# Attention backward on one core: giving nine of the dk stores another distribution over the DMA engines

## The chip, the core and the metric

The kernel runs on one core of one Trainium2 chip. The metric is the device time of one execution in microseconds (us). The core has 16 DMA engines, which all its loads and stores share. A DMA issued by GpSimd (POOL in the profile) goes through the "software" queue q0, one issued by SyncE (SP) through the "hardware" queue q1.

## The reference

Attention with one query per head, and its gradients, in bf16: 2 x 32 = 64 heads, 8192 keys, D = 128.

```python
def _fwd_reference(q, k, v):                 # q: 2,32,1,128   k, v: 2,32,8192,128
    scale = q.shape[-1] ** -0.5
    scores = jnp.einsum("bhqd,bhkd->bhqk", q, k) * scale
    p = _softmax(scores, axis=-1)
    return jnp.einsum("bhqk,bhkd->bhqd", p, v)

def reference(q, k, v, grad_out):            # returns out, dq, dk, dv
    out, vjp = jax.vjp(_fwd_reference, q, k, v)
    return (out, *vjp(grad_out))
```

Per head, k and v are read and dk and dv written, 2 MB each: 537 MB in all. With 128 partitions, one partition's share of a head (a "row") is 64 keys x 128 x 2 bytes = 16 KB, contiguous in memory.

## The kernel before

PE transposes and multiplies the k and v tiles of one head while the next heads are loaded. DVE overwrites a tile with its gradient, and the tile is then stored from where it lies. Loads are issued by SyncE, stores by GpSimd (in the last head in small pieces by SyncE). Twelve tiles are in use in turn, so a load waits for the store that empties its tile.

```python
FIRST = 6
SPREAD = range(4, 60, 7)
...
load_eng = nc.sync
store_eng = nc.gpsimd
...
    def by_rows(eng, dst, src, rows):
        p = 0
        for m in rows:
            pin(eng.dma_start(out=dst[p : p + m], in_=src[p : p + m], max_dma_last_dim=NT * D))
            p += m
...
        if r0:                         # r0 = FIRST for q
            pin(store_eng.inc_swdge_sem([], [], mode="reset_dge_cursor"))
            pin(store_eng.dma_start(out=qd_nat[:r0, w, :], in_=rows[:r0], max_dma_last_dim=D))
        pin(load_eng.dma_start(out=qd_nat[r0:BH, w, :], in_=rows[r0:BH]))
...
            if w == 0 and i in SPREAD:                       # dk of heads 4, 11, ... 53
                by_rows(store_eng, dst, h.tile[w], (P - 2, 2))
            else:
                eng = load_eng if len(ends) > 1 else store_eng
                pin(eng.dma_start(out=dst[:, b0:b1, :], in_=h.tile[w][:, b0:b1, :]))
```

In the packet records a plain store of 128 rows gives each engine 8 rows, and the eight spread stores divide 126 rows by 14 engines, so that two engines get next to nothing. Where a copy over fewer than 16 engines begins is kept by a cursor of the software queue (the prediction quotes the rule). The program resets it at the start and moves it to 6 by a load of six rows.

## Time and profile before

| | before |
|---|---|
| time, median of 4 runs | 1280.99 us (1280.43 to 1281.8) |
| span of the profiled run | 1280.2 us |
| PE busy | 1190.2 us, 93% |
| last two stores issued (compute over) | 1270.29 us |
| DMA, mean over the span | 421 GB/s |

The page gives busy time per engine. In rows of digits each digit is a fortieth of the span, in tenths busy. A window line gives a stretch, its length, the busy time of PE, PEld (weight loads), DVE, ACT and POOL with instruction counts, the PE clock, the DMA share (1.00 is all 16 engines) and GB/s. A DMA share of 0.06 is one engine.

### The profile page before, as it was taken

The page shows a single profiled execution, that of the slowest core. Times are in us where ns is not written, and L with a number is a line of the kernel's source. Part 1 is how long each engine was busy: PE and PEld are TensorE (multiplying, and loading weights), DVE is VectorE, ACT ScalarE, POOL GpSimd, SP SyncE. Part 2 cuts the span into 40 slices and gives each one's busy share as a digit, 9 for nine tenths or more (in the row PEclk, how much of TensorE's full clock was granted, in tenths as well). Part 3 has the DMA queues.
Part 4 walks back from the last instruction along what each step waited for, and adds up shares of the span by engine and source line. Part 5 has one row for each costly group of instructions (what it writes and reads, how often), then busy time and mean ns, then how long its engine had stood idle before and what let it go on. Part 6 is the DMA issues. An engine that isn't in the chain of part 4 may idle for free.

```text
span 1280.2 us, 32473 instructions
## 1 busy us (share of the span) xinstructions
PE 1190.2 (93%) x14148; PEld 810.6 (63%) x14148; DVE 1025.8 (80%) x2256; ACT 975.3 (76%) x641; POOL 76.0 (6%) x143
## 2 busy tenths in 40 slices
PE   6999999999999999999999999999999999999994
PEld 5666666666666666666666666666666666666662
DVE  2888887888877888888888878788778888888885
ACT  6777777778777777777777777787777777777771
POOL 0000000000000000000000000000000000000000
PEclk9999999999999999999999999999999999999996
DMA  9999999999999999999999999999999999999996
GB/s 392 423 428 428 428 427 429 430 426 429 427 430 425 414 427 429 428 423 428 428 429 419 425 428 426 427 421 427 427 423 421 427 429 428 420 425 428 428 411 273
DMA packets 40155, 539.03 MB, mean 421 GB/s; under 512 B 5196, under 2 KB 5196, under 8 KB 6476
## 3 DMA queue, kind: packets, MB, share of 16 engines
q1 hardware_dynamic: 20172, 272.70, 50.1%
q0 software_dynamic: 19840, 264.25, 49.0%
q8 instruction: 110, 1.80, 0.5%
q14 instruction: 33, 0.27, 0.1%
HBM read 268.47 MB, written 268.47 MB: 419 GB/s over the span
## 4 chain that ended last, share of the span: by engine, by line
PE 59%; DVE 16%; ACT 10%; issue 10%; DMA 4%; POOL 0%; SPq 0%; ACTq 0%; POOLq 0%; DVEq 0%
PE tp L194 24%; PE acc L372 15%; ACT ev L196 9%; PE raw L208 9%; DVE kvt L427 6%; PE sw L228 4%; DVE sel L395 4%; DMA out_dram<-kvt 3%; DVE rows L221 3%; PE sw L315 3%; PE sw L178 2%; PE acc L409 2%; ACT E_f L271 1%; DVE sel L389 1%; DVE E_pad L280 1%
## 5 line engine op out<-in xcount | busy, mean ns | idle before, releaser
L196 ACT COPY ev<-tp 128x2048 bf16<-128x2048 bf16 x512 | 954.5, 1865 | 275.6 <-PE tp L194 268.9
L427 DVE TENSOR_TENSOR kvt<-qb,pair 128x2048 bf16<-128x2048 bf16 x512 | 616.8, 1216 | 0.2
L194 PE MATMUL tp<-ident_bf,kvt 128*128 128x128 bf16 x8192 | 544.4, 220 | 0.0
L194 PEld LDWEIGHTS <-kvt 128*128 128x128 bf16 x8192 | 482.4, 99 | 81.6 <-issue 80.7
L208 PE MATMUL raw<-ev,qdT 128*32 128x512 bf16 x2048 | 205.2, 391 | 1.5 <-ACT ev L196 1.5
L372 PE MATMUL acc<-kvt,E_pad 128*64 128x512 bf16 x1024 | 160.2, 393 | 24.5 <-DVE E_pad L280 24.5
L372 PE MATMUL acc<-kvt,dS_pad 128*64 128x512 bf16 x1024 | 159.8, 393 | 0.1
L228 PEld LDWEIGHTS sw<-sel,rows 128*128 128x128 f32 x1024 | 124.7, 192 | 52.4 <-DVE sel L395 25.9
L395 DVE SCALAR_TENSOR_TENSOR sel<-acc,diag,sel 128x128 f32<-128x128 f32 x384 | 134.8, 351 | 13.6
L208 PEld LDWEIGHTS <-qdT 128*32 128x32 bf16 x2048 | 53.1, 93 | 136.6 <-issue 131.8
L228 PE MATMUL sw<-sel,rows 128*128 128x16 f32 x1024 | 137.1, 266 | 0.0
L445 POOL DMA_DIRECT2D out_dram<-kvt x118 | 63.3, 536 | 1094.0 <-DVE kvt L427 555.7
L221 DVE COPY rows<-raw 128x512 f32<-128x512 f32 x128 | 88.6, 692 | 22.4 <-PE raw L208 22.4
L280 DVE CAST E_pad<-E_f 128x64 bf16<-128x64 f32 x64 | 12.5, 195 | 80.3 <-ACT E_f L271 80.3
L372 PEld LDWEIGHTS <-E_pad 128*64 128x64 bf16 x1024 | 36.1, 108 | 49.9 <-DVE E_pad L280 35.7
L178 PE MATMUL sw<-ident_bf,qdT 128*128 128x128 bf16 x128 | 28.5, 223 | 38.2 <-DVE mp L240 38.2
L246 DVE TENSOR_REDUCE gm<-sw 1x1 f32<-1x128 f32 x64 | 17.9, 279 | 55.4 <-PE sw L244 55.4
L315 PEld LDWEIGHTS sw<-ld,ones 128*128 128x128 f32 x256 | 38.1, 188 | 29.7 <-issue 15.0
L372 PEld LDWEIGHTS <-dS_pad 128*64 128x64 bf16 x1024 | 36.4, 108 | 22.3 <-DVE dS_pad L358 1.0
L315 PE MATMUL sw<-ld,ones 128*128 128x1 f32 x256 | 49.1, 261 | 0.0
L409 PE MATMUL acc<-ones,sel 128*128 128x1 f32 x256 | 43.3, 239 | 5.3 <-DVE sel L395 5.3
L389 DVE TENSOR_SCALAR sel<-acc,diag 128x128 f32<-128x128 f32 x128 | 43.8, 342 | 0.0
(49 smaller groups left out, 377.1 us busy)
## 6 DMA issues: line engine op xcount, KB each, us to landing
out_dram<-kvt POOLq DMA_DIRECT2D x118, 2048.0 KB, 40.6
kvt<-in_v_dram SPq DMA_DIRECT2D x64, 2048.0 KB, 19.1
kvt<-in_k_dram SPq DMA_DIRECT2D x63, 2048.0 KB, 19.4
out_dram<-kvt POOLq DMA_DIRECT2D x8, 2016.0 KB, 44.9
out_dram<-kvt SPq DMA_DIRECT2D x8, 512.0 KB, 10.9
kvt<-in_k_dram SPq DMA_DIRECT2D x2, 512.0 KB, 4.3
kvt<-in_k_dram SPq DMA_DIRECT2D x1, 1024.0 KB, 6.9
out_dram<-kvt POOLq DMA_DIRECT2D x8, 32.0 KB, 44.3
```

The costliest lines, as they stand in the source:

```text
L194: pin(nc.tensor.transpose(tp[:, t, :], src[:, c * CH + t, :], ident_bf[:]))
L196: pin(nc.scalar.copy(out=ev[:], in_=tp[:]))
L208: nc.tensor.matmul(h.raw[g * SW : (g + 1) * SW, :], lhsT=qdT[:, w, q0 : q0 + SW], rhs=ev[:, g * QT : (g + 1) * QT, :].rearrange("p n d -> ...
L221: pin(nc.vector.tensor_copy(out=h.rows[:], in_=h.raw[:]))
L228: nc.tensor.matmul(h.score[w].rearrange("p (n t) -> p n t", t=QT)[:, :, t], lhsT=h.rows[:, t * P : (t + 1) * P], rhs=sel4[:].rearrange("p ...
L315: nc.tensor.matmul(out, lhsT=ones[:].to_broadcast([P, P]), rhs=col, start=True, stop=True)
L372: nc.tensor.matmul(h.acc[w][g : g + CW, :], lhsT=wts[:, n0 : n0 + CW], rhs=rows[:, n0 : n0 + QT, :].rearrange("p n d -> p (n d)"), start=( ...
L389: nc.vector.tensor_scalar(out=h.sel[:], in0=block, scalar1=diag[:, 0:1], scalar2=None, op0=ALU.mult)
L395: nc.vector.scalar_tensor_tensor(out=h.sel[:], in0=block, scalar=diag[:, b : b + 1], in1=h.sel[:], op0=ALU.mult, op1=ALU.add,)
L409: nc.tensor.matmul(h.acc[w][:, 0:1], lhsT=h.sel[:], rhs=ones[:], start=True, stop=True)
L427: nc.vector.tensor_tensor(out=h.tile[w][:, n0 : n0 + CH, :].rearrange("p n (e t) -> p n e t", t=2), in0=h.qb[w][:] .rearrange("p (e t) -> ...
L445: pin(eng.dma_start(out=dst[:, b0:b1, :], in_=h.tile[w][:, b0:b1, :]))
```

## The change

Its intent, as its short description says, is to take work from one engine, number 4, in seven stores (120 rows over 15 engines), and from engines 7 and 8 in two late ones (112 rows). SyncE stores the seven rows left over. The last row goes in pieces of 9 and 8 columns (3 and 2 in the last store), evidently chosen so that 15 + 9 + 8 = 32 brings the cursor back (in the last, 15 + 3 + 2 = 20 would set it to 9, from where 14 engines would leave out 7 and 8).

```diff
-FIRST = 6
-SPREAD = range(4, 60, 7)
+FIRST = 5
+ONE = {4: 9, 12: 9, 20: 9, 28: 9, 36: 9, 44: 9, 52: 3}
+TWO = (57, 61)
...
-            if w == 0 and i in SPREAD:
-                by_rows(store_eng, dst, h.tile[w], (P - 2, 2))
+            if w == 0 and i in ONE:
+                by_rows(store_eng, dst, h.tile[w], (P - 8,))
+                by_rows(load_eng, dst, h.tile[w], (7,), P - 8)
+                a = 2 * ONE[i]
+                for eng, cols in (
+                    (store_eng, slice(0, a - 1, 2)),
+                    (store_eng, slice(1, a - 2, 2)),
+                    (load_eng, slice(a - 1, NT)),
+                ):
+                    pin(eng.dma_start(out=dst[P - 1 :, cols, :], in_=h.tile[w][P - 1 :, cols, :]))
+            elif w == 0 and i in TWO:
+                by_rows(store_eng, dst, h.tile[w], (P - 16, 2))
+                by_rows(load_eng, dst, h.tile[w], (7, 7), P - 14)
```

(by_rows also gets a first row as a parameter; lines are joined here.)

More of the change, by code (lines that the diff above doesn't have):

```diff
@@ L83, in slot_of, with by_rows @@
         return n if n < NTILE else slot_of(i - NTILE // 2, 1 - w)
-    def by_rows(eng, dst, src, rows):
-        p = 0
+    def by_rows(eng, dst, src, rows, p=0):
         for m in rows:
@@ L440, in outer @@
             dst = (dv_v if w else dk_v)[i]
-            if w == 0 and i in SPREAD:
-                by_rows(store_eng, dst, h.tile[w], (P - 2, 2))
+            if w == 0 and i in ONE:
[7 more added lines that the diff above has]
+                ):
+                    pin(
+                        eng.dma_start(
+                            out=dst[P - 1 :, cols, :], in_=h.tile[w][P - 1 :, cols, :]
+                        )
+                    )
+            elif w == 0 and i in TWO:
+                by_rows(store_eng, dst, h.tile[w], (P - 16, 2))
+                by_rows(load_eng, dst, h.tile[w], (7, 7), P - 14)
             else:
```

## The prediction

> **What bounds the kernel now.** I read the page's busy shares first, then the windows of 19.4 us (one head each), then the end of the run in small windows, then the issues and SyncE's waits.
>
> ```profile
> PE 1190.2 (93%) x14148; PEld 810.6 (63%) x14148; DVE 1025.8 (80%) x2256; ACT 975.3 (76%) x641; POOL 76.0 (6%) x143
> ...
> PEclk9999999999999999999999999999999999999996
> DMA  9999999999999999999999999999999999999996
> ```
>
> PE and the DMA engines are both full until the last slice. The windows decide between them (columns: stretch, its length, busy us of PE, PEld, DVE, ACT, POOL, clock, DMA share, GB/s):
>
> ```profile
> 75.40:94.80 19.40, 18.43 (x223) 12.58 (x221) 15.94 (x36) 15.19 (x11) 1.06 (x2) 1.00 1.01 428
> ...
> 405.90:425.40 19.50, 18.54 (x225) 12.59 (x221) 16.04 (x36) 15.29 (x11) 1.13 (x2) 1.00 1.00 409
> ...
> 1203.20:1222.60 19.40, 18.44 (x225) 12.59 (x221) 15.93 (x36) 15.18 (x11) 1.06 (x2) 1.00 1.01 430
> ```
>
> PE does the same 18.4 us of work in every window, also where the DMA rate drops to 409 GB/s: PE never waits for data. The chain of waits agrees: its marker, one 1.86 us eviction per head, recurs every 19.445 us. So compute takes about 17 + 64 x 19.445 = 1261.5 us and a short tail, and no DMA change can shorten that. A head moves 8.39 MB, which at 19.445 us asks for 431 GB/s; the DMA engines give about 427. They fall behind a little all the way, and what is left of that is paid at the end:
>
> ```profile
> 1268.00:1270.00 2.00, 0.89 (x3) 0.63 (x3) 0.92 (x3) 0.00 (x0) 0.00 (x0) 0.50 0.96 389
> 1270.00:1272.00 2.00, 0.01 (x1) 0.00 (x0) 0.35 (x2) 0.00 (x0) 0.00 (x0) 0.50 0.54 217
> 1272.00:1274.00 2.00, 0.00 (x0) 0.00 (x0) 0.00 (x0) 0.00 (x0) 0.00 (x0) 0.50 0.47 182
> 1274.00:1276.00 2.00, 0.00 (x0) 0.00 (x0) 0.00 (x0) 0.00 (x0) 0.00 (x0) 0.50 0.08 30
> 1276.00:1278.00 2.00, 0.00 (x0) 0.00 (x0) 0.00 (x0) 0.00 (x0) 0.00 (x0) 0.50 0.06 25
> ...
> 1270.29 1.88 SPq L528 DMA_DIRECT2D out_dram<-nat  x2
> ```
>
> Compute is over at 1270.3, when SyncE issues the last two small stores. From 1274 to 1278 the DMA share is 0.06, which is one engine of 16 (1/16 = 0.0625). **One straggling DMA engine sets the end.** Its last packet ends at 1278.15 in the packet records, the span 2.0 us later.
>
> To know the engines I chained the packet records: they name no engine, but a 16 KB packet takes 611 ns and the next on the same engine starts 607 ns after it, so sixteen chains can be followed. This is my reconstruction (chains can swap where two coincide), but it fits every packet count. It says:
> - In each of the eight spread stores 14 chains carry 18 packets of 8 KB (nine rows) and two carry only 4-byte ones, then one row each. So these two are relieved by 7 rows, 8 times.
> - Exactly one engine is slow from the first store on: its packets take 13 to 60 ns too long, 44 us in the run. It is one of the relieved two. The other one has 27 us of long packets, but in bursts, when it has run ahead and starts a new load at once; an ordinary engine has 4 to 14.
> - The 110 fetches of PE instructions (queue q8, about 0.96 us each) go in turn to 8 engines, 14 each, 13 us. The slow engine is not among them, the other relieved one is.
> - Idle time up to the end: slow engine 12 us, the other relieved one 20, the engines without fetches 6 to 15, those with fetches mostly under 2. The straggler is a fetching engine with 13 us of long packets; its sisters end at 1273.3 to 1274.4.
>
> **What the Trainium skill says.** "DMA: Bandwidth & Descriptors", section "Why a DMA increments its semaphore by 16 and not by 1": a copy uses the largest k up to 16 that divides both sides' slowest dimension; the hardware queue uses the lowest-numbered k engines, the software queue k consecutive ones from a round-robin cursor; and some direct software copies take all 16 regardless. The trace agrees for 126 rows: 14 chains, two left out. No trace yet shows 120, 112 or a copy of nine columns. The same page, "Issuing engines are not separate DMA queues": moving a store to SyncE adds no bandwidth; here both queues fill the same 16 chains. The same page, "Latency and other measured facts", calls engines 7 and 15 the usual slow ones; here one engine is slow, and the change's own choice says that its number is 4.
>
> **The change part by part,** in rows of 16 KB against an even split, 0.611 us a row, if the cursor moves as the rule says.
> - Before: the first small load of 6 rows puts the cursor at 6; 126 rows go to 6-15 and 0-3, 2 rows to 4 and 5. Eight times: engines 4 and 5 have -56 rows, the others +8.
> - After, seven stores: cursor 5, 120 rows on 15 engines, all but 4; then 9 and 8 column pieces bring it round (15 + 9 + 8 = 32) to 5. Seven rows by SyncE go to engines 0-6, the rest of the last row (12 to 15 KB) to engine 0. Engine 4: 7 x (-8 + 1) = -49. Engines 1-3, 5, 6: +7. Engine 0: about +12. Others 0.
> - Two stores of 112 rows: the title wants 7 and 8 left out; by the rule 16 divides 112, so I count 7 rows on each engine, two rows to two engines, 14 by SyncE to 0-6: +2 for 0-6, -1 or -2 for 7-15. With 7 and 8 left out it would be -14 for these two and 4 for 0-6.
>
> Change against before: engine 4 +9 rows (5.5 us of its 12 idle). Engine 5 +65 rows, 40 us, against 20 us idle plus some 20 us of burst waits (27 less an ordinary 7): it just fits. Engines 7-15: 9 or 10 rows less, -6 us. Engines 1-3 and 6 +1 row, 0 about +6: up to 4 us, inside the idle of engines without fetches. A fetching engine at +1 row or engine 5 ends near 1274; if the straggler is among 7-15, it ends near 1272. The floor is the last small store: on engines that keep up it lands at 1273.2. So the last packet is at about 1274, the span 1276, and with the 0.5 us that timed runs are above this span, **1276.7 us**. All gain is in the 4 us of the lone engine.
>
> Costs: GpSimd issues 16 more small copies; it is 6% busy, so they are hidden. The 256-byte pieces are 17 packets a store, nothing. SyncE's rows stand in its queue between two loads, behind a wait for an earlier store:
>
> ```profile
> SPq L100 <- DMA out_dram<-kvt: 1136.8, 116, 27.5
> ...
> out_dram<-kvt POOLq DMA_DIRECT2D x118, 2048.0 KB, 40.6
> kvt<-in_v_dram SPq DMA_DIRECT2D x64, 2048.0 KB, 19.1
> ```
>
> They are issued a store's 40 us later than now and land behind the load just queued (19 us), so the next load starts about 10 us later in nine heads. The engines stay busy with the store queue, which has several stores waiting. The last load (head 63) is issued at 1211.5, lands at about 1230 and is first used at about 1241; issued at about 1222 it lands near 1233, since nothing is queued before it. No PE stall.
>
> **The rivals.** First, *the cursor does not move as planned*. A nine-column copy has a single counting dimension, and the skill's exception (all 16 engines) may apply; then the pieces leave the cursor alone, and the left-out engine walks 4, 3, 2, 1, 0, 15, 14. Engine 4 has then +1 row instead of -56: 57 rows at 0.63 us are 36 us, less 12 idle: 24 us behind 1273, a span near 1299 with one engine alone for over 20 us. For it: the old code split rows in two to get this behaviour, the new pieces don't. Against: 9 + 8 and 3 + 2 columns make sense only if the author had seen the cursor move by them. I give it 0.35 to 0.4. Second, *SyncE's queue becomes the wait*: a load late by more than its lead stalls PE, which then moves the whole end. The lead of the last load is about 10 us; I expect 0 to 4 us, 1277 to 1281. Third, *engine 5 or a sister becomes the straggler*, if the burst waits were not slack: up to 20 us, again near 1295; the trace speaks against it, as its first 397 us have only 2 us of long packets. Fourth, *all balanced but nothing gained*: some engine among 0-6 carries what the straggler carried, 1280.
>
> **Range and chances.** With 0.6 the plan works: 1275 to 1280. With 0.4 one engine is overloaded: 1290 to 1300. The middle of this mixture is 1278; eight in ten need both modes, 1274.5 to 1299.5. Two per cent faster (1255) is below the compute floor of 1275: 0.01. Slower than 1306 needs an overload and a PE stall together: 0.04.
>
> **What would show it.** Right: PE 18.4 us in every window, compute over at 1270.3, no window at a share of 0.06 after 1274, in each of the seven stores one chain with 4-byte packets only, and it is the slow one. Wrong: the share stays at 0.06 for 20 us (an engine overloaded; the chain's packets of over 611 ns tell whether it is engine 4), or PE windows under 18 us (loads late), or compute's last store after 1271.

## The result, and the profile after

| | before | after |
|---|---|---|
| time, median of 4 runs | 1280.99 us | 1304.08 us (1301.69 to 1304.16) |
| ratio | | 1.0175 (95%: 1.0158 to 1.0193) |
| span of the profiled run | 1280.2 us | 1302.4 us |

Ratios are computed from means: the mean time of one kernel's fast runs over that of the other's in the same rounds, so not quite the ratio of the medians. The changed kernel is slower by 23 us, inside two per cent and outside the predicted range.

The page of after, the lines that answer to those of before:

```profile
PE 1194.4 (92%) x14148; PEld 812.0 (62%) x14148; DVE 1025.4 (79%) x2256; ACT 975.3 (75%) x641; POOL 79.5 (6%) x151
...
PEclk9999999999999999999999999999999999999995
DMA  9999999999999999999999999999999999999965
GB/s 391 421 428 429 427 425 428 428 428 428 419 429 428 427 426 419 428 429 425 422 414 429 429 424 425 410 428 427 426 427 425 429 425 429 417 420 426 415 238 205
```

PE does the same work. The DMA rate is that of before until the last two slices. Windows of before that the prediction did not show:

```profile
1222.60:1242.10 19.50, 18.53 (x225) 12.59 (x221) 16.03 (x36) 15.28 (x11) 1.06 (x2) 1.00 0.96 406
1242.10:1261.50 19.40, 16.56 (x136) 9.62 (x132) 16.28 (x37) 7.58 (x6) 1.06 (x2) 0.82 0.83 352
1261.50:1280.90 19.40, 2.58 (x14) 1.42 (x14) 7.60 (x15) 0.00 (x0) 0.00 (x0) 0.57 0.55 224
```

The same windows of after, and its end:

```profile
1203.20:1222.60 19.40, 18.02 (x219) 12.52 (x217) 15.33 (x36) 14.77 (x11) 1.06 (x2) 1.00 1.01 429
1222.60:1242.10 19.50, 18.54 (x225) 12.59 (x221) 16.02 (x36) 15.29 (x11) 1.06 (x2) 1.00 0.86 350
1242.10:1261.50 19.40, 14.44 (x151) 9.45 (x148) 12.35 (x29) 10.65 (x6) 1.83 (x3) 0.91 0.85 327
1261.50:1280.90 19.40, 15.28 (x107) 8.29 (x106) 16.60 (x35) 4.04 (x4) 0.55 (x1) 0.77 0.59 237
...
1285.00:1290.00 5.00, 0.32 (x1) 0.13 (x1) 0.40 (x3) 0.00 (x0) 0.00 (x0) 0.50 0.30 114
1290.00:1295.00 5.00, 0.00 (x0) 0.00 (x0) 0.00 (x0) 0.00 (x0) 0.00 (x0) 0.50 0.06 27
1295.00:1300.00 5.00, 0.00 (x0) 0.00 (x0) 0.00 (x0) 0.00 (x0) 0.00 (x0) 0.50 0.06 26
```

Two things are seen. From 1290 to 1300 one engine works alone. And PE, which before had 2.58 us left to do after 1261.5, has 15.28 us left now, so it has lost time. The group of PE's transposes says to whom (page; the last column is PE's idle time just before them and its releaser), before and then after:

```profile
L194 PE MATMUL tp<-ident_bf,kvt 128*128 128x128 bf16 x8192 | 544.4, 220 | 0.0
```

```profile
L194 PE MATMUL tp<-ident_bf,kvt 128*128 128x128 bf16 x8192 | 545.4, 220 | 12.7 <-DMA kvt<-in_v_dram 11.0
```

PE waits 11.0 us for late v tiles. The last two stores are issued at 1285.70 (timeline of SyncE in after), 15.4 us later than before:

```profile
1285.70 3.07 SPq L543 DMA_DIRECT2D out_dram<-nat  x2
```

So of the 22 us between the spans some 15 are late compute. The rest is a longer tail behind it, most of it the lone engine.

**Which engine.** I chained the packet records of after into sixteen engines as for before. A left-out engine shows as a chain that carries only 4-byte packets of a 120-row store. In the seven stores it was a different chain each time. The first was the slow chain. The fifth was the one that carries SyncE's 12 KB rest of the last row, which is engine 0 if the hardware queue uses the lowest engines. The first five lie among the chains that carry the 256-byte column pieces, the last two do not. That is the walk 4, 3, 2, 1, 0, 15, 14: the cursor moves by 15 in each store and not at all by the pieces, whose data landed on the same nine and eight chains every time. The slow engine was relieved once and then carried one row above even in each of six stores. This is a reconstruction, and it ends at 1235 us. So I tested it.

### The profile page after: what moved, and what is told of

It reads as the page before. It is cut to its first block, busy times and chain, and to the rows that moved or that the text cites. A ratio compares the mean times of both kernels' runs of the same rounds, so it can differ in the third digit from the quotient of the medians.

```text
span 1302.4 us, 32523 instructions
## 1 busy us (share of the span) xinstructions
PE 1194.4 (92%) x14148; PEld 812.0 (62%) x14148; DVE 1025.4 (79%) x2256; ACT 975.3 (75%) x641; POOL 79.5 (6%) x151
## 4 chain that ended last, share of the span: by engine, by line
PE 55%; DVE 15%; DMA 10%; ACT 9%; another core or an unknown queue 6%; issue 2%; SPq 0%; ACTq 0%; DVEq 0%
PE tp L194 23%; PE acc L372 14%; DMA kvt<-in_v_dram 9%; PE raw L208 8%; ACT ev L196 8%; DVE kvt L427 6%; PE sw L228 4%; DVE sel L395 4%; DVE rows L221 3%; PE sw L315 2%; PE sw L178 2%; PE acc L409 1%; ACT E_f L271 1%; DVE sel L389 1%
## 5 line engine op out<-in xcount | busy, mean ns | idle before, releaser
L372 PEld LDWEIGHTS <-dS_pad 128*64 128x64 bf16 x1024 | 36.6, 108 | 22.3 <-issue 0.9
```

The lines of the kernel that those rows point to most:

```text
L372: nc.tensor.matmul(h.acc[w][g : g + CW, :], lhsT=wts[:, n0 : n0 + CW], rhs=rows[:, n0 : n0 + QT, :].rearrange("p n d -> p (n d)"), start=( ...
```

## Experiments

Each of the four calls ran on another chip (14, 6, 4 and 12), with runs of before on the same chip. So between calls the ratios can be compared better than the medians.

**Call 1: the cursor.** The tool is a tiny software copy from q into unused memory. It has two counting dimensions, as the first small load has, and so should take as many engines as it has rows and move the cursor:

```diff
+    moved = nc.dram_tensor("moved", (512, D), BF16, kind="Internal").ap()
+    def move_cursor(m):
+        pin(store_eng.dma_start(out=moved[put[0] : put[0] + m, : D // 2], in_=rows[:m, : D // 2], max_dma_last_dim=D // 4))
+        put[0] += m
```

e1_back: after the pieces of each 120-row store, tiny copies of 9 and 8 rows.

```diff
+                move_cursor(9); move_cursor(8)
```

> The changed kernel with two tiny software copies more after each of the seven 120-row stores, of 9 and of 8 rows of q into unused memory, each with two counting dimensions, as the first small load has them. Theory A (the column pieces do not move the software queue's cursor, so the left-out engine walks 4, 3, 2, 1, 0, 15, 14): 9 + 8 = 17 slots undo the walk by one, the same engine is left out in all seven stores, and the time falls from 1304 to 1276 - 1280 us, with compute over near 1270 and no lone engine for longer than 4 us. Rival B (SyncE's rows delay the loads, or engine 5 is the straggler, whatever the cursor does): stays at 1300 - 1306. Rival C (the pieces do move the cursor by 17): 17 more spoil a plan that worked, another walk, 1300 or more, with the left-out chain moving on by one each time.

e2_sixteen, its control:

```diff
+                move_cursor(8); move_cursor(8)
```

> As e1_back, but the two tiny copies have 8 and 8 rows: 16 slots, which bring a cursor of 16 back to where it was. It is the control for what the tiny copies do by themselves. Theory A: the walk of the changed kernel stays, 1302 - 1306 us. If the tiny copies helped by anything else than the cursor, e1_back and e2_sixteen would be equal.

e4_five:

```diff
-FIRST = 5
+FIRST = 6
+                move_cursor(9); move_cursor(8)
```

> As e1_back, but the first small load has 6 rows in place of 5, so that the one engine left out seven times is the next one, engine 5. Theory A with the slow engine being number 4: engine 4 has one row more per store than an even share (SyncE's rows begin at engine 0) and is skipped in none, against one skip in the changed kernel: 8 rows or 5 us more, 1305 - 1312 us. If any engine left out seven times would do, or if engine 5 were the straggler: 1276 - 1285.

e3_plain:

```diff
-            if w == 0 and i in ONE:
+            if False:
...
-            elif w == 0 and i in TWO:
+            elif False:
```

> All dk stores as plain 128-row copies over 16 engines, by the software queue, no rows on SyncE. Theory A: in the changed kernel the slow engine ended with about as many rows as an even split gives it, so without any relief the time is about the same, 1300 - 1306 us. Rival B (SyncE's rows in the queue of the loads cost the 20 us): without them 1280 or less.

| | median | ratio to before (95%) |
|---|---|---|
| e1_back | 1292.44 us | 1.0093 (1.0051 to 1.0134) |
| e2_sixteen | 1306.72 us | 1.0199 (1.0164 to 1.0234) |
| e4_five | 1316.9 us | 1.0278 (1.0248 to 1.0308) |
| e3_plain | 1293.86 us | 1.0103 (1.0074 to 1.0133) |

e1_back and e2_sixteen differ by one slot of the cursor per store, and by 14.3 us. In the chains of e1_back one and the same engine, the slow one, is left out in all seven stores. In e2_sixteen it is a different one from store to store, and only the first is the slow one. So **the pieces do not move the cursor, and that costs 14 us**: theory A's cause holds. e4_five is slower again: the same relief given to engine 5 does not help. The loss against e2_sixteen is 10 us, twice the 5 us that I expected from after.

A count that needs no chains agrees. The slow engine shows in 8 KB packets of 313 to 341 ns, where 309 is usual. The seven 120-row stores have 0, 10, 8, 6, 13, 10 and 12 of these in after, 0, 10, 10, 5, 14, 13 and 11 in e2_sixteen, at most 2 each in e1_back, and 5 to 15 each in e4_five.

PE's waits tell where the late compute comes from. e3_plain has no rows on SyncE and no relief; e1_back has all of SyncE's rows and the relief (pages, e3_plain first):

```profile
L194 PE MATMUL tp<-ident_bf,kvt 128*128 128x128 bf16 x8192 | 544.4, 220 | 11.5 <-DMA kvt<-in_v_dram 8.6
```

```profile
L205 PE MATMUL tp<-ident_bf,kvt 128*128 128x128 bf16 x8192 | 544.2, 220 | 1.5 <-DMA kvt<-in_v_dram 1.5
```

So the late loads come with the missing relief, and SyncE's rows do not make them. The last two stores are issued at 1282.55 in e3_plain and at 1272.35 in e1_back.

But two expectations failed. e1_back should have reached 1276 to 1280 and stopped at 1292, where again one engine works alone (windows of e1_back, whose trace is of its slowest run, 1297.29):

```profile
1285.00:1290.00 5.00, 0.00 (x0) 0.00 (x0) 0.00 (x0) 0.00 (x0) 0.00 (x0) 0.50 0.06 27
1290.00:1295.00 5.00, 0.00 (x0) 0.00 (x0) 0.00 (x0) 0.00 (x0) 0.00 (x0) 0.50 0.05 20
```

In the chains this last engine is not the slow one. It is one that fetches PE instructions (a fetching engine, for short) and also carries SyncE's rows. And e3_plain, with nothing done for the slow engine, is 10 us faster than the changed kernel, though by rows the slow engine has nearly the same share in both (one row more in the changed kernel). Something in the change costs by itself.

**Call 2: what else costs.** e5_back_no112:

```diff
 # e1_back, and
-TWO = (57, 61)
+TWO = ()
```

> e1_back without the two 112-row stores (plain 128-row stores in their place). e1_back showed the same chain left out in all seven stores and still took 1292 us, with a fetching engine that carries SyncE's rows as the straggler. Theory T (the two 112-row stores overload it: 14 rows by SyncE to seven engines, each a row or two more than even): about 1278 - 1284. Theory S (SyncE's seven rows and the last row in the seven 120-row stores are the cost): 1287 - 1293, at most 3 us below e1_back.

f1_soft8 (a copy of a 9 and an 8 is 17 slots, one more than a round):

```diff
+TWO = ()
                 by_rows(store_eng, dst, h.tile[w], (P - 8,))
-                by_rows(load_eng, dst, h.tile[w], (7,), P - 8)   # and the pieces
+                move_cursor(9); move_cursor(8)      # every second store: move_cursor(8)
+                by_rows(store_eng, dst, h.tile[w], (8,), P - 8)
+                move_cursor(8)                      # every second store: 9 and 8
```

> The seven stores as 120 rows without the slow engine, but the last 8 rows go by the software queue too, alternately to engines 5-12 and 12-15, 0-3, with tiny copies that set the cursor; no rows on SyncE, no 112-row stores. The slow engine has 56 fewer rows, as in the kernel before, the others 3 to 7 more. Theory S (SyncE's rows and pieces made the straggler of e1_back): 1275 - 1278 us, a little under before. Theory 5 (the second relieved engine of the kernel before, number 5, needed its relief, or 120-row stores disturb by themselves): 1288 - 1296.

f2_walk_soft8:

```diff
-                by_rows(load_eng, dst, h.tile[w], (7,), P - 8)   # and the pieces
+                by_rows(store_eng, dst, h.tile[w], (8,), P - 8)
+                move_cursor(8)
```

> The changed kernel with only this edit: the last 8 rows of each of the seven stores go by the software queue (8 engines from the cursor on, then one tiny copy of 8 rows), not by SyncE and in pieces. The left-out engine walks on by one per store as in the changed kernel, and the slow engine has the same rows as there. Theory S (SyncE's rows and pieces cost some 10 us on top of the lost relief, which is why the changed kernel is 10 us slower than plain stores): 1293 - 1297. If only the lost relief counts: 1302 - 1306, as the changed kernel.

e2_nopieces:

```diff
-                by_rows(load_eng, dst, h.tile[w], (7,), P - 8)   # and the pieces
+                by_rows(load_eng, dst, h.tile[w], (8,), P - 8)
```

> The changed kernel with the last 8 rows of the seven stores whole by SyncE: no pieces. The walk of the left-out engine stays, since the pieces do not move the cursor. Theory A: 1300 - 1306, and the left-out chains as in the changed kernel. If the pieces moved the cursor, or cost by themselves: the walk changes and the time falls by more than 5 us.

| | median | ratio to before (95%) |
|---|---|---|
| e5_back_no112 | 1285.22 us | 1.0033 (1.0004 to 1.0061) |
| f1_soft8 | 1280.5 us | 1.0000 (0.9981 to 1.0018) |
| f2_walk_soft8 | 1310.0 us | 1.0235 (1.0216 to 1.0253) |
| e2_nopieces | 1308.75 us | 1.0216 (1.0201 to 1.0232) |

Without the two 112-row stores e1_back gains 0.6%, 7 to 8 us, with intervals that overlap. That is theory T's number; its reason, SyncE's 14 rows, does not survive call 4. e5_back_no112 still varies from 1280.8 to 1289.2, and its trace is of the fastest run. In its chains the two that end last, at 1277.2 and 1275.6 against 1274.3 or less for the others, are the two fetching engines that carry SyncE's rows. With those rows spread by the software queue (f1_soft8) the time is that of before: neither the 1275 to 1278 of theory S nor the 1288 or more of theory 5. f2_walk_soft8 refutes theory S as I had put it: with the walk in place, taking SyncE's rows and the pieces away gains nothing (1310, not 1295). e2_nopieces shows that taking the pieces away gains nothing and that they do not make the walk: without them the left-out chain still changes from store to store (chains valid to 828 us, five stores; the slow one in the first only), and the time is 1308.75, above the 1300 to 1306 that I expected.

The chains of f1_soft8 and e1_back also tell which engines fetch. In f1_soft8, five fetching chains carry extra rows only from the stores that used engines 5 to 12, two only from those that used 12 to 15 and 0 to 3, and one from both (12). In e1_back, two fetching chains carry SyncE's rows (engines 0 to 6), and six carry no column piece (9 to 15). Together these leave 5, 6, 9 to 12 and two of 13 to 15.

**Call 3: the fetching engines, and the 112-row stores by themselves.** h1_spare (n > 0 is a tiny copy of n rows, n < 0 stores that many rows):

```diff
 # TWO = (); after the 120 rows, in turn
+                (3, -2, 14, -2, 7, -4, 9, 8)   or   (11, -5, 12, -3, 2)
```

> Seven stores of 120 rows without the slow engine, and their last 8 rows by the software queue on engines that fetch no PE instructions: alternately 2 + 2 rows on 7 and 8 and 4 on 0-3, and 5 rows on 15, 0-3 and 3 on 0-2, with tiny copies that set the cursor. No rows on SyncE, no 112-row stores. From f1_soft8 and e1_back I infer that the fetching engines are 5, 6 and 9-14 (their chains carry the rows of those copies). Theory F (a fetching engine is the straggler of before, with 13 us of fetches and 8 rows above even): with 0 rows above even it ends 4.9 us sooner, so 1276 - 1278 us in the timed runs, under before. Rival (compute and the last stores set the end, or long packets come from anything uneven): 1280, as before and f1_soft8.

h2_fetching:

```diff
 # TWO = (); after the 120 rows
+                (5, -6, 6, -2, 14)
```

> The counterpart of h1_spare: the last 8 rows of each of the seven stores go to the eight fetching engines, 9-14 and 5, 6, one row each: 7 rows above even for each, 0 for the others; the slow engine is relieved as there. Theory F: 4 us slower than h1_spare, 1280 - 1283. Rival: no difference to h1_spare.

g1_no112:

```diff
 # the changed kernel, and
-TWO = (57, 61)
+TWO = ()
```

> The changed kernel with plain stores in place of its two 112-row stores, nothing else. e5_back_no112 was 7 us faster than e1_back. If these two stores cost the same here: 1296 - 1299, near the plain kernel's 1294, which has the same rows on the slow engine. If the end is set by the slow engine's rows alone: 1302 - 1305.

g2_before_112:

```diff
 # the kernel before, and
+            elif w == 0 and i in (57, 61):
+                by_rows(store_eng, dst, h.tile[w], (P - 16, 2))
+                by_rows(load_eng, dst, h.tile[w], (7, 7), P - 14)
```

> The kernel before with the change's two 112-row stores in heads 57 and 61 and nothing else of it. If these stores cost by themselves (long packets, the 14 rows that wait in SyncE's queue): 1286 - 1292. If they cost only where an engine is behind already: 1279 - 1283.

| | median | ratio to before (95%) |
|---|---|---|
| h1_spare | 1294.43 us | 1.0100 (1.0078 to 1.0121) |
| h2_fetching | 1280.39 us | 0.9991 (0.9971 to 1.0011) |
| g1_no112 | 1299.85 us | 1.0138 (1.0116 to 1.0159) |
| g2_before_112 | 1288.13 us | 1.0044 (1.0021 to 1.0067) |

The 112-row stores cost 0.4% (6 us) in the kernel before and as much in the changed one (1.0175 without this edit, 1.0138 with it, some 5 us). h1_spare is the largest miss: what should have been the best was 14 us slower than its counterpart. In its trace the DMA engines have gaps after a store with eight tiny and partial copies (windows of h1_spare, where the share otherwise is 1.00 or more):

```profile
463.83:483.27 19.44, 18.48 (x225) 12.59 (x223) 15.97 (x36) 15.22 (x11) 2.76 (x5) 1.00 0.73 287
1105.50:1124.95 19.45, 18.49 (x225) 12.61 (x223) 15.99 (x37) 15.24 (x11) 3.63 (x7) 1.00 0.66 248
```

GpSimd's timeline just before the first gap (start, length, instruction; in brackets how long GpSimd stood idle before it, and what released it):

```profile
439.63 0.55 POOL L89 DMA_DIRECT2D out_dram<-kvt  x1
440.55 0.58 POOL L125 DMA_DIRECT2D moved<-in_q_dram  x1 [0.37 <-DMA out_dram<-kvt]
450.29 0.59 POOL L89 DMA_DIRECT2D out_dram<-kvt  x1 [9.16 <-DMA out_dram<-kvt]
459.96 0.58 POOL L125 DMA_DIRECT2D moved<-in_q_dram  x1 [9.07 <-DMA out_dram<-kvt]
474.15 0.57 POOL L125 DMA_DIRECT2D moved<-in_q_dram  x1 [13.61 <-DMA moved<-in_q_dram]
```

GpSimd's copies use eight semaphores in turn. The copy at 459.96 took the one of the store issued at 426.3, eight copies earlier, which landed at 459.67. So in this program at most eight software copies are in flight, however small. A burst of nine behind stores that take 40 us makes GpSimd wait for each store in front of it, and the queue runs dry.

**Call 4: the two mechanisms by themselves, and the plan with few copies.** These four are to settle what the 112-row stores and h1_spare had left open. j1_112_soft:

```diff
 # the kernel before, and
+            elif w == 0 and i in (57, 61):
+                by_rows(store_eng, dst, h.tile[w], (P - 16, 16))
```

> The kernel before with heads 57 and 61 stored as 112 rows and then 16 rows, both by the software queue; no rows on SyncE. g2_before_112 (112 and 2 rows by the software queue, 14 by SyncE) took 1288 against 1282 us, with packets of those stores and of their neighbours twice their usual length in the last 100 us. If the 112-row copies (7 rows to an engine) make these long packets: again 1286 - 1290, with some 100 us of long packets after 1200. If SyncE's 14 rows, which stand before nothing but still wait in its queue, did it: 1280 - 1283 and under 20 us of long packets after 1200.

j2_burst:

```diff
 # the kernel before, and after the 126 + 2 rows
+                for _ in range(8):
+                    move_cursor(16)
```

> The kernel before with eight tiny software copies (16 rows of 128 bytes, which leave the cursor where it is) after each of its eight spread stores. h1_spare had eight or nine software copies per store, its DMA engines all had gaps after them (in one window of 19.4 us the share fell to 0.66), and GpSimd waited there up to 13 us for copies to land. If a burst of software copies by itself starves the queue: 1290 - 1300, with such gaps after every second store or more and GpSimd waits for DMA of over 100 us in total. If the rows of h1_spare were the cause: 1280 - 1284.

j3_six:

```diff
-SPREAD = range(4, 60, 7)
+SPREAD = range(4, 60, 11)
```

> The kernel before with six spread stores in place of eight (heads 4, 15, 26, 37, 48, 59). Slow engine: 14 rows or 8.5 us more, against 12 us idle; all others 2 rows or 1.2 us less. If a fetching engine with 8 rows above even is the straggler of before: 1279 - 1280.5, about 1 us faster; if the last stores or compute set the end: no change.

j4_few:

```diff
 # the changed kernel with TWO = (); after the 120 rows, in place of SyncE's 7 rows and the pieces
+                move_cursor(11)
+                by_rows(store_eng, dst, h.tile[w], (4,), P - 8)
+                move_cursor(2)
+                by_rows(load_eng, dst, h.tile[w], (4,), P - 4)
```

> h1_spare's aim with four software copies per store in place of eight: 120 rows without the slow engine, a tiny copy of 11 rows, 4 rows on 15, 0, 1, 2, a tiny copy of 2 rows that brings the cursor back to 5, and the last 4 rows by SyncE on 0-3. No fetching engine has a row above even. If the burst of copies made h1_spare slow: 1276 - 1280. If these rows or anything else did: 1288 or more.

| | median | ratio to before (95%) |
|---|---|---|
| j1_112_soft | 1288.84 us | 1.0070 (1.0043 to 1.0097) |
| j2_burst | 1313.86 us | 1.0255 (1.0232 to 1.0279) |
| j3_six | 1280.64 us | 0.9998 (0.9977 to 1.0019) |
| j4_few | 1276.37 us | 0.9968 (0.9946 to 0.9989) |

j1_112_soft: without any row on SyncE the cost is there in full, so it is the 112-row software copies. The window of head 61's store (to be held against 0.83 and 352 GB/s of before):

```profile
1242.10:1261.50 19.40, 17.27 (x155) 10.60 (x153) 16.28 (x37) 8.95 (x7) 1.11 (x2) 0.84 0.86 295
```

The engines are as busy and move less: 352 / 0.83 = 424 GB/s per full share before, 295 / 0.86 = 343 here. In the packet records it is long packets: the time beyond 611 ns (16 KB), 309 ns (8 KB) and the like, summed over the run from 1200 us on, is 7 us before, 101 in g2_before_112 and 85 in j1_112_soft; in e1_back many 8 KB packets of head 61's store took about 0.63 us. A late store in 8 KB packets does not do it by itself: j3_six (below) has a store of 126 + 2 rows in head 59, only some 24 us of long packets after 1200, and the time of before. Why 7 rows to an engine do it is not shown. The Trainium skill, "DMA: Bandwidth & Descriptors", section "The descriptor swizzle", says that in a 128-partition transfer each engine writes one SBUF port, which has eight partitions. 112 rows may not be dealt out like that, but that is no sufficient reason: nine rows to an engine, as in the store of 126, cannot be either. No run here shows ports.

j2_burst: the burst alone costs 33 us, more than the 10 to 20 that I expected, with gaps after seven of the eight spread stores and this wait of GpSimd (waits of POOL; total, times, longest):

```profile
POOL moved L124 <- DMA out_dram<-kvt: 381.3, 41, 15.3
```

The same run's row of DMA shares on the page shows the gaps as eights:

```profile
DMA  9999999998999899989999899989999999989998
```

j3_six is inconclusive: 1 us expected, an interval of 5 us.

j4_few is the plan carried out: the slow engine left out in all seven stores, the eight rows on engines that fetch nothing, four software copies per store, no 112-row store. It takes 1276.37 us, 0.3% less than the kernel before (0.9946 to 0.9989; under the two per cent that count as a difference). Its end (windows):

```profile
1268.00:1270.00 2.00, 0.31 (x2) 0.32 (x2) 1.53 (x5) 0.00 (x0) 0.00 (x0) 0.50 1.00 399
1270.00:1272.00 2.00, 0.59 (x3) 0.31 (x2) 0.57 (x3) 0.00 (x0) 0.00 (x0) 0.50 0.41 162
1272.00:1274.00 2.00, 0.00 (x0) 0.00 (x0) 0.00 (x0) 0.00 (x0) 0.00 (x0) 0.50 0.09 16
1274.00:1276.00 2.00, 0.00 (x0) 0.00 (x0) 0.00 (x0) 0.00 (x0) 0.00 (x0) 0.50 0.00 0
```

There is no lone engine. The 16 engines' parts of the last store land within 0.2 us of each other (within 5.6 us before). In its chains one engine, the slow one, is left out seven times, and the rows lie on five chains without fetches. What remains is the compute.

## Why the prediction was wrong

**The step that failed is "if the cursor moves as the rule says".** I gave it 0.6 and rival 1, "the cursor does not move as planned", 0.35 to 0.4. Rival 1 is what happened, down to the walk of the left-out engine (e1_back against e2_sixteen: 14.3 us). I had the evidence in hand: the old code split its rows in two, and the new pieces have one counting dimension. I overruled it with a guess at what the author must have seen. What was seen, the same nine and eight chains each time and a cursor that stays, fits the exception of the Trainium skill, "DMA: Bandwidth & Descriptors", section "Why a DMA increments its semaphore by 16 and not by 1" (some direct software copies take all 16 engines); the page does not say which copies.

The cursor is not all of it. With the cursor put right, the planned layout took 1292.44 us (e1_back), not 1276.7. Three runs lead from after back to before: the cursor put right takes the ratio from 1.0175 to 1.0093 (e1_back), plain stores in place of the 112-row ones to 1.0033 (e5_back_no112), the last rows by the software queue in place of SyncE's rows and pieces to 1.0000 (f1_soft8). That is about 10, 8 and 4 us. The intervals of e1_back and e5_back_no112 overlap, and so do those of e5_back_no112 and f1_soft8. Other runs show the first two steps (e2_sixteen; g2_before_112 and j1_112_soft); the last is not shown.

**Rival 1's size was too small.** It said a span near 1299, with one engine alone for over 20 us and no PE stall. Measured: 1302.4, alone for some 13 us from about 1288, compute over 15 us late. That the two numbers are as close as they are is partly luck: the term left out and a lone time too long nearly cancel. The term left out is that an engine far behind holds back loads, since a load waits for the whole store that empties its tile. The last engine's part of a store landed up to 30.8 us behind the fifteenth's in after and 22.3 in e3_plain, against 10.5 in before and 2.6 in f1_soft8, and PE waited 11.0 us for v tiles. "No PE stall" was derived for SyncE's queue alone; it held in the runs where the engines kept up (0.0 us in f1_soft8 and j4_few). The prediction took an overload and a PE stall together for an event of 0.04 (over 1306); here the one brought the other.

**The 112-row stores were mis-sized.** I counted rows: "+2 for 0-6", some 1 us. They cost 6 us in the kernel before (g2_before_112) and 8 (j1_112_soft), by packets up to twice as long. That they would leave 7 and 8 out I doubted rightly: in after they went over all 16 chains, 7 rows each.

**Borne out, but by another plan:** that all there was to gain is the 4 us of the lone engine. j4_few took 1276.37 us where the main line said 1276.7. That they agree so closely is luck: j4_few has other rows on other engines, and its span is 1274.7 where the prediction said 1276. The account of a straggler among the fetching engines is supported and not shown: with the same relief, rows on those engines give 1280.39 (h2_fetching), rows off them 1276.37 (j4_few). But the two also differ in their software copies (six and four a store) and ran in different calls; their ratios to before, 0.9991 and 0.9968, have intervals that overlap.

**Rivals 2 to 4.** Rival 3, engine 5 or a sister as straggler, is partly true: even with the cursor put right, the two fetching engines under SyncE's rows end last (the trace of e5_back_no112). Rival 2, SyncE's queue, was no cause by itself: taking its rows out does not help while the walk is there (f2_walk_soft8), and PE waits for tiles without them too (e3_plain) and hardly with them (e1_back). Rival 4, balanced at 1280, is f1_soft8.

**Two slips in the sums.** "GpSimd issues 16 more small copies": it issues 8 more (POOL x151 against x143 on the pages), since before had eight small ones. And a timed run is 1.8 us above its own span (1276.46 and 1274.7 in j4_few); the 0.5 us compares the span of one run with the median of others. Neither changes the argument.

**Open.** The changed kernel without its 112-row stores (g1_no112, ratio 1.0138) is still 0.35%, some 4 us, slower than plain stores (e3_plain, 1.0103), though the slow engine has no more rows there (their intervals overlap, and they ran on different chips); and f2_walk_soft8 and e2_nopieces, which remove parts of the change, are 4 to 6 us slower than it, not faster. In e2_nopieces the extra time is late compute: PE waits 25.5 us before its transposes, and the last stores are issued at 1302.78. I have no run that explains either.

## What to carry to other kernels

When work is moved off one DMA engine, count engine by engine what each carries (rows, fetches, slow packets) and check in the packet records that the copies really went where the rule of k and cursor puts them; a copy with one counting dimension did not. An extra copy can cost more than its bytes: in this program small software copies took the place of stores among the eight that may be in flight (33 us in j2_burst), and a split of 7 rows to an engine came with packets up to twice as long. An engine that falls behind cost twice here, at the end by itself and before that through the buffers that it kept full.

## What the Trainium skill lacked or had wrong

- "DMA: Bandwidth & Descriptors", "Why a DMA increments its semaphore by 16 and not by 1": it says that some direct software copies take all 16 engines, but not which, nor what they do to the cursor. Here pieces of 9, 8, 3 and 2 columns (one counting dimension) put data on the same chains each time and did not move it: one slot per store given back was worth 14.3 us. Copies of 120, 8 or 4 rows with each row in two parts, and tiny ones of 2 to 14 rows, followed the rule, as far as the left-out engine shows it.
- Same page, "Latency and other measured facts", names engines 7 and 15 as the usual slow ones: here exactly one engine was slow, 13 to 60 ns a 16 KB packet, 44 us in the run of before, and leaving out number 4 (by the rule of the cursor) relieved it (e1_back) while leaving out number 5 did not (e4_five). It was the same number on all four chips of the calls: where number 4 is left out, no 120-row store has more than 3 packets of 313 to 341 ns (e1_back, f1_soft8, h1_spare, j4_few).
- No page I read has it: the 110 fetches of PE instructions went to eight of the 16 engines only (here 5, 6, 9 to 12 and two of 13 to 15, by inference), about 14 each of 0.96 us.
- No page I read has it: this program's software copies share eight semaphores, so that a burst of eight tiny ones after each of eight stores cost 33 us (j2_burst).
- No page I read has it: software copies of 112 rows, 7 to an engine, ran at 343 GB/s per full share against 424 (j1_112_soft), and two of them cost 6 to 8 us.
